# Padding every matmul of a fused attention and mixer kernel to the full TensorE array

## The chip, the cores and the metric

One core of a Trainium2 chip runs the program. The metric is the time of one execution on the device in microseconds (us). A TensorE matmul here is two instructions: a weight load of the stationary operand (`lhsT`; the profile's PEld, LDWEIGHTS) and a MATMUL that streams the moving operand (`rhs`) through the array. The profile writes the part of the array that an instruction uses as rows*columns: `128*64` is a stationary operand with 128 contraction rows and 64 columns.

## The reference

Batch 8, 8 heads, 576 positions, head size 64; then a mixer over positions of rank 32 and one over channels, 512 to 2048 to 512.

```python
cum  = np.cumsum(np.maximum(s, 0.0), axis=-1)
bias = -(cum[:, :, :, None] - cum[:, :, None, :])
scores = np.where(causal, -1e9, q @ k^T / sqrt(64) + np.minimum(bias, 0.0))
x = softmax(scores) @ v                       # heads side by side: (8, 576, 512)
u = x + (x.transpose(0, 2, 1) @ U @ V).transpose(0, 2, 1)   # U 576x32, V 32x576
out = u + np.maximum(u @ w_ch1, 0.0) @ w_ch2
```

## The kernel before

The 64 heads are worked in 32 pairs (four pairs a batch). The 576 positions make four key tiles of 128 and a tail tile of 64, which is where the part-filled arrays come from.

For pair n the program has these stages, each a generator that yields between pieces:

- `transposes(n+1)`: q and k (72 positions by 128 columns at a time) are transposed on TensorE (L159, stationary operand 72*128) into PSUM, and VectorE copies them into one of three `slot` tiles (L164). Four more rows of a slot, which carry the cumulative bias, come by DMA from `rows_hbm` (L151). A stationary operand of the scores has therefore 64 + 4 = 68 rows.
- `scores(n)`: for each of two heads nine matmuls (L180) make the score tiles transposed, keys on partitions: four diagonal blocks into `diag`, the tail block (keys and queries 512 to 575, stationary operand 68*64) into `tail`, and the blocks away from the diagonal into `far` and `mid`. ScalarE takes the exponential into `pT` (L191, L200, L204; L206 for both tails), VectorE masks the diagonal (L192, L212).
- `values(n-1)`: 15 matmuls a head (L235) multiply pT by v. v carries a 65th column of ones, so that the sums of the softmax come along. In the last row of blocks the one with j = 2 has a stationary operand of 128*64 and the one with j = 4 one of 64*64. VectorE divides (L244, L245) into `x_sb`.
- `seqmix(b)`, after each batch: U^T x in five matmuls (L259, stationary operand 128*32 four times, then 64*32), a copy to `ux` (L267), then x^T by multiplication with the identity (L272, 128*128) plus ux by V into the same PSUM tile (L280, 32*128), a copy to `uT` (L288); for the last 64 positions the same with 64*128 (L292) and 32*128 (L300) in turn, four of each, and L308.
- `chanmix(g)`, for 512 tokens: 64 matmuls 128x512 (L321), each four followed by a relu on ScalarE (L328), then 64 more (L334), the residual (L345), the copy out (L354) and the store. It is cut into pieces of four matmuls, 32 of them, and `step_fill` puts one piece behind each yield of the stages above: a pair gives 8 yields, `seqmix` 6 more a batch. Batch 0 has nothing to be filled with; the last two `chanmix` run alone at the end.

Loads of q, k, v and the weights (U_sb, V_sb, w1, w2) are DMAs issued by GpSimd in program order: q and k of batch 0, v of batch 0, all weights, then q, k and v of the next batches. At the very start GpSimd also fills constants (L68 to L100), and VectorE makes the bias rows out of s (L64 to L76), which go to HBM and back. PSUM tiles come from two pools of four, `pscore` and `pwork`. The order of each engine's instructions is fixed when the program is built.

Of the kernel before, what the change touches and what calls it, by code (L numbers as in the profile page):

```python
# [20 lines left out]
def kernel(  # L21
# [12 lines left out]
    nc = tc.nc  # L34
    B, H, S, D = q.shape
    assert (B, H, S, D) == (8, 8, 576, 64)
    DM = H * D
    FF = 4 * DM
    R = moe_U.shape[1]
    scale = 1.0 / (D ** 0.5)  # L40
    BH = B * H
# [4 lines left out]
    KA = D + 4  # L46
    NF = FF // 128

    consts = ctx.enter_context(tc.tile_pool(name="consts", bufs=1))
    loads = ctx.enter_context(tc.tile_pool(name="loads", bufs=2))  # L50
    work = ctx.enter_context(tc.tile_pool(name="work", bufs=2))
# [6 lines left out]
    def pwork():  # L58
        return ps_w.tile([128, 512], FP32, tag="w", name="pwork")


    s_sb = consts.tile([BH, S], FP32)
    nc.sync.dma_start(out=s_sb, in_=s.rearrange("b h s -> (b h) s"))
    nc.vector.tensor_scalar(s_sb, s_sb, 0.0, 1.0 / scale, op0=ALU.max, op1=ALU.mult)  # L64
    cum = consts.tile([BH, S], FP32)
    nc.vector.tensor_tensor_scan(cum, s_sb, s_sb, 0.0, op0=ALU.add, op1=ALU.max)
    rows = consts.tile([BH, 4, 2, S], BF16)
    nc.gpsimd.memset(rows[:, 0:3, 0, :], 1.0)  # L68
    nc.gpsimd.memset(rows[:, 3, 1, :], 1.0)
    rest = s_sb  # L70
# [6 lines left out]
    rows_hbm = nc.dram_tensor("rows_hbm", (4, BH, 2, S), BF16, kind="Internal").ap()  # L77
    nc.sync.dma_start(out=rows_hbm.rearrange("r n c s -> n r c s"), in_=rows)

    identity = consts.tile([128, 128], BF16)  # L80
    make_identity(nc, identity)

    keep = consts.tile([128, 4, 128], BF16)
    nc.gpsimd.memset(keep, 3.0e38)
    nc.gpsimd.affine_select(
        out=keep,
        in_=keep,
# [9 lines left out]
    v_slots = []  # L97
    for i in range(3):
        vt = consts.tile([128, 5, H, D + 1], BF16, name=f"v_slot{i}")
        nc.gpsimd.memset(vt[:, :, :, D : D + 1], 1.0)  # L100
        v_slots.append(vt)

    def load_qk(b, cuts):
# [22 lines left out]
    load_v(0)  # L126
    w1_sb = consts.tile([128, 4, FF], BF16)
    w2_sb = consts.tile([128, NF, DM], BF16)
    U_sb = consts.tile([128, 5, R], BF16)
    V_sb = consts.tile([R, S], BF16)  # L130

    def load_weights():
        nc.gpsimd.dma_start(
            out=U_sb[:, :4, :], in_=moe_U[:512].rearrange("(kt kp) r -> kp kt r", kp=128)
        )
        nc.gpsimd.dma_start(out=U_sb[:64, 4, :], in_=moe_U[512:576])
        nc.gpsimd.dma_start(out=V_sb, in_=moe_V)
        nc.gpsimd.dma_start(out=w1_sb, in_=moe_w_ch1.rearrange("(kt kp) n -> kp kt n", kp=128))
        nc.gpsimd.dma_start(out=w2_sb, in_=moe_w_ch2.rearrange("(kt kp) n -> kp kt n", kp=128))

    NSLOT = 3
    slots = [consts.tile([128, 2, 2, S], BF16, name=f"slot{i}") for i in range(NSLOT)]
    uT = consts.tile([128, 4, B * S], BF16)

    pT_of, x_of = {}, {}


    def transposes(n):
        b, hp = divmod(n, PB)
        slot = slots[n % NSLOT]  # L150
        nc.sync.dma_start(out=slot[D:KA], in_=rows_hbm[:, ds(2 * n, 2)])  # L151
        for hh in range(2):
            h = 2 * hp + hh
            tp = pwork().bitcast(BF16)[:, : 2 * 4 * TP].rearrange(
                "p (c t m) -> p c t m", c=2, t=4
            )
            for c, src in enumerate((q_t[b], k_t[b])):
                for t2 in range(4):
                    nc.tensor.transpose(  # L159
                        tp[:, c, t2, :], src[:, h, ds(t2 * 128, 128)], identity[:TP, :TP]  # L160
                    )
            dst = slot[0:D, hh].rearrange("p c (m t two) -> p c m t two", t=4, two=2)
            for par in range(2):
                nc.vector.tensor_copy(  # L164
                    dst[:, :, :, :, par],
                    tp[par * D : par * D + D].rearrange("p c t m -> p c m t"),
                )
            yield

    def scores(n):  # L170
        slot = slots[n % NSLOT]
        pT = work.tile([128, 2, 1600], BF16, tag="pT", name="pT")
        pT_of[n] = pT
        tail = pscore()
        for hh in range(2):
            qT = slot[0:KA, hh, 0, :]
            kT = slot[0:KA, hh, 1, :]

            def mm(dst, j, lo, hi):
                nc.tensor.matmul(  # L180
                    dst,
                    lhsT=kT[:, ds(j * 128, min(128, S - j * 128))],
                    rhs=qT[:, lo:hi],
                    start=True,
                    stop=True,
                )

            diag = pscore()
            for j in range(4):
                mm(diag[:, ds(j * 128, 128)], j, j * 128, j * 128 + 128)  # L190
            nc.scalar.activation(pT[:, hh, 0:512], diag, EXP, scale=scale)  # L191
            nc.vector.tensor_tensor(  # L192
                pT[:, hh, 0:512], pT[:, hh, 0:512], keep.rearrange("p a b -> p (a b)"), op=ALU.min
            )
            mm(tail[:64, ds(hh * 64, 64)], 4, 512, S)
            yield
            far = pscore()
            mm(far[:, 0:448], 0, 128, S)
            mm(far[:, 448:512], 3, 512, S)
            nc.scalar.activation(pT[:, hh, 512:1024], far, EXP, scale=scale)  # L200
            mid = pscore()
            mm(mid[:, 0:320], 1, 256, S)
            mm(mid[:, 320:512], 2, 384, S)
            nc.scalar.activation(pT[:, hh, 1024:1536], mid, EXP, scale=scale)  # L204
            if hh == 1:
                nc.scalar.activation(  # L206
                    pT[:64, :, 1536:1600],
                    tail[:64, 0:128].rearrange("p (a b) -> p a b", a=2),
                    EXP,
                    scale=scale,  # L210
                )
                nc.vector.tensor_tensor(  # L212
                    pT[:64, :, 1536:1600], pT[:64, :, 1536:1600], keep[:64, 0:2, 0:64], op=ALU.min
                )
            yield


    def place(j, i):
        if i == j:
            return 128 * j if j < 4 else 1536  # L220
        return {0: 512, 1: 1024, 2: 1344, 3: 960}[j] + 128 * (i - j - 1)

    def values(n):
        b, hp = divmod(n, PB)
        if hp == 0:
            x_of[b] = work.tile([128, 5, DM], BF16, tag="x_sb", name="x_sb")
        x_sb, pT, vt = x_of[b], pT_of.pop(n), v_slots[b % 3]
        for hh in range(2):
            h = 2 * hp + hh
            po = pwork()[:, : 5 * (D + 1)].rearrange("p (i d) -> p i d", i=5)  # L230
            for i in range(5):
                for j in range(i + 1):
                    kk = 64 if j == 4 else 128
                    mq = 64 if i == 4 and j in (2, 4) else 128
                    nc.tensor.matmul(  # L235
                        po[:mq, i, :],
                        lhsT=pT[:kk, hh, ds(place(j, i), mq)],
                        rhs=vt[:kk, j, h, :],
                        start=(j == 0),
                        stop=(j == i),  # L240
                        skip_group_check=True,
                    )
            rec = work.tile([128, 5, 1], FP32, tag="rec", name="rec", bufs=4)
            nc.vector.reciprocal(rec, po[:, :, D : D + 1])  # L244
            nc.vector.tensor_tensor(  # L245
                x_sb[:, :, ds(h * D, D)],
                po[:, :, 0:D],
                rec.to_broadcast([128, 5, D]),
                op=ALU.mult,
            )  # L250
            yield


    def seqmix(b):
        x_sb = x_of.pop(b)
        up = pwork()
        for t in range(5):
            kk = min(128, S - t * 128)
            nc.tensor.matmul(  # L259
                up[:R, :],  # L260
                lhsT=U_sb[:kk, t, :],
                rhs=x_sb[:kk, t, :],
                start=(t == 0),
                stop=(t == 4),
            )
        ux = work.tile([R, DM], BF16, tag="ux", name="ux")
        nc.vector.tensor_copy(ux, up[:R, :])  # L267
        yield
        for dt in range(4):
            ut = pwork()  # L270
            for t in range(4):
# [3 lines left out]
                    rhs=identity,  # L275
# [15 lines left out]
        for dt in range(4):  # L291
            nc.tensor.matmul(  # L292
                ut[:, ds(dt * 64, 64)],
                lhsT=x_sb[:64, 4, ds(dt * 128, 128)],
                rhs=identity[:64, :64],
                start=True,
                stop=False,
                skip_group_check=True,
            )
            nc.tensor.matmul(  # L300
                ut[:, ds(dt * 64, 64)],
                lhsT=ux[:, ds(dt * 128, 128)],
                rhs=V_sb[:, 512:S],
                start=False,
                stop=True,
                skip_group_check=True,
            )
# [116 lines left out]
```

## Time and profile before

| | |
|---|---|
| median of 3 runs | 488.96 us (487.77 to 490.62) |
| the profiled execution | 485.0 us, span 483.3 us |
| TensorE matmul busy | 452.3 us, 94% of the span, 3608 matmuls |
| VectorE busy | 232.1 us, 48% |
| ScalarE busy | 192.4 us, 40% |
| GpSimd busy | 58.9 us, 12% |
| mean granted TensorE clock | 0.982 of full speed |

Read it with care in one place: the end of a matmul is modelled and matmuls overlap, so the busy share of TensorE does not tell how much of the time data stream through the array. The distance from the start of one matmul to the start of the next tells more.

### The profile page before, as it was taken

To read this page: it belongs to the slowest core of one execution; us is meant where nothing else is said; L and a number is where in the kernel's file an instruction comes from. 1 tells how busy PE (TensorE), PEld (TensorE's weight loads), DVE (VectorE), ACT (ScalarE), POOL (GpSimd) and SP (SyncE) were. 2 spreads that over 40 slices of the span, in tenths; PEclk is the share of its full clock that TensorE was granted. 3 is DMA by queue.
4 is the path that set the end of the run, shared out by engine and by line. 5 is a ranking of instruction groups with operands and counts; after the bars stand their busy time and mean duration, and the time that the engine had idled before them with its cause. 6 is when DMAs were issued, how large, how long until landed. Compare 5 with 4: busy or idle time off the path is not lost.

```text
span 483.3 us, 8414 instructions
## 1 busy us (share of the span) xinstructions
PE 452.3 (94%) x3608; PEld 255.9 (53%) x3608; DVE 232.1 (48%) x444; ACT 192.4 (40%) x369; POOL 58.9 (12%) x80
## 2 busy tenths in 40 slices
PE   1195999999999999999999999999999999999996
PEld 1073645555555555555556555555555555444443
DVE  6363755555455544556455644555555543401101
ACT  1064236532562266324742165326632662061430
POOL 9720341003000301021100310000000000000000
PEclk9999999999999989998999799999999999999999
DMA  5999996518071536127431806110011000101101
GB/s 83 189 210 191 111 127 31 83 55 87 3 101 46 72 25 88 37 54 64 60 67 46 72 4 99 46 46 2 3 47 46 1 0 24 45 22 45 43 23 65
DMA packets 59221, 29.74 MB, mean 62 GB/s; under 512 B 42320, under 2 KB 53616, under 8 KB 59184
## 3 DMA queue, kind: packets, MB, share of 16 engines
q0 software_dynamic: 53392, 18.44, 45.3%
q1 hardware_dynamic: 5792, 10.77, 6.4%
q8 instruction: 28, 0.46, 0.4%
q14 instruction: 9, 0.07, 0.1%
HBM read 37.58 MB, written 10.03 MB: 99 GB/s over the span
## 4 chain that ended last, share of the span: by engine, by line
PE 89%; DMA 7%; POOL 2%; DVE 1%; issue 0%; POOLq 0%
PE pwork L321 28%; PE pwork L334 27%; PE pscore L180 11%; PE pwork L235 10%; DMA q_sd<-in_q_dram 6%; PE pwork L159 3%; PE pwork L259 2%; PE pwork L272 2%; PE pwork L280 2%; PE pwork L345 2%; DMA v_slot_93<-in_v_dram 2%; PE pwork L292 1%; PE pwork L300 1%; POOL k_sd L109 1%; POOL q_sd L109 1%
## 5 line engine op out<-in xcount | busy, mean ns | idle before, releaser
L321 PE MATMUL pwork<-uT,w_sb 128*128 128x512 bf16 x576 | 146.7, 391 | 0.0
L334 PE MATMUL pwork<-w_sb,hT 128*128 128x512 bf16 x576 | 144.4, 380 | 0.0
L328 ACT ACTIVATE hT<-pwork 128x512 bf16<-128x512 f32 x144 | 86.4, 600 | 106.1 <-PE pwork L321 105.5
L191 ACT ACTIVATE pT<-pscore 128x512 bf16<-128x512 f32 x64 | 38.4, 600 | 145.8 <-issue 89.5
L321 PEld LDWEIGHTS <-w_sb 128*128 128x128 bf16 x576 | 52.1, 100 | 51.2 <-issue 5.0
L334 PEld LDWEIGHTS <-hT 128*128 128x128 bf16 x576 | 49.2, 98 | 45.2 <-issue 1.1
L235 PEld LDWEIGHTS <-pT 128*128 128x128 bf16 (+2 forms) x960 | 54.3, 102 | 24.0 <-issue 0.4
L354 DVE COPY o_sb<-pwork 128x512 f32<-128x512 f32 x36 | 24.9, 692 | 75.7 <-PE pwork L345 75.7
L244 DVE RECIPROCAL rec<-pwork 128x5 f32<-128x5 f32 x64 | 12.3, 195 | 87.5 <-PE pwork L235 87.3
L192 DVE TENSOR_TENSOR pT<-pT,keep 128x512 bf16<-128x512 bf16 x64 | 26.3, 414 | 47.5 <-ACT pT L191 47.5
L200 ACT ACTIVATE pT<-pscore 128x512 bf16<-128x512 f32 x64 | 38.1, 595 | 20.0 <-PE pscore L180 19.0
L180 PE MATMUL pscore<-slot_118 68*128 68x128 bf16 (+5 forms) x198 | 28.5, 266 | 10.7 <-DMA slot_118<-rows_hbm 10.7
L204 ACT ACTIVATE pT<-pscore 128x512 bf16<-128x512 f32 x64 | 38.2, 597 | 0.3 <-PE pscore L180 0.2
L164 DVE COPY slot_119<-pwork 64x576 bf16<-64x576 bf16 x44 | 35.1, 799 | 6.2 <-PE pwork L159 4.6
L164 DVE COPY slot_118<-pwork 64x576 bf16<-64x576 bf16 x44 | 35.2, 799 | 4.5 <-PE pwork L159 3.1
L159 PE MATMUL pwork<-identity,q_sd 72*128 72x72 bf16 x256 | 20.9, 213 | 15.4 <-DMA q_sd<-in_q_dram 15.4
L164 DVE COPY slot_120<-pwork 64x576 bf16<-64x576 bf16 x40 | 32.0, 801 | 4.4 <-PE pwork L159 3.1
L159 PEld LDWEIGHTS <-q_sd 72*128 72x128 bf16 x256 | 17.4, 108 | 27.8 <-DMA q_sd<-in_q_dram 16.1
L245 DVE TENSOR_TENSOR x_sb<-pwork,rec 128x320 bf16<-128x320 f32 x64 | 31.1, 490 | 2.0
L180 PE MATMUL pscore<-slot_119 68*128 68x128 bf16 (+5 forms) x198 | 28.6, 263 | 0.8 <-DVE slot_119 L164 0.8
L180 PEld LDWEIGHTS <-slot_118 68*128 68x128 bf16 (+1 forms) x198 | 16.5, 105 | 23.0 <-issue 12.4
L235 PE MATMUL pwork<-v_slot_93,pT 128*128 128x65 bf16 (+1 forms) x360 | 27.2, 214 | 0.0
(59 smaller groups left out, 333.9 us busy)
## 6 DMA issues: line engine op xcount, KB each, us to landing
out_dram<-o_sb SPq DMA_DIRECT2D x36, 256.0 KB
w_sb<-in_moe_w_ch_dram POOLq DMA_DIRECT2D x2, 2048.0 KB, 19.6
q_sd<-in_q_dram POOLq DMA_DIRECT2D x7, 576.0 KB, 7.9
k_sd<-in_k_dram POOLq DMA_DIRECT2D x7, 576.0 KB, 11.0
v_slot_93<-in_v_dram POOLq DMA_DIRECT2D x12, 128.0 KB, 7.8
v_slot_95<-in_v_dram POOLq DMA_DIRECT2D x12, 128.0 KB, 6.1
v_slot_97<-in_v_dram POOLq DMA_DIRECT2D x8, 128.0 KB, 9.1
q_sd<-in_q_dram POOLq DMA_DIRECT2D x4, 144.0 KB, 5.0
```

The costliest lines, as they stand in the source:

```text
L159: nc.tensor.transpose(tp[:, c, t2, :], src[:, h, ds(t2 * 128, 128)], identity[:TP, :TP])
L164: nc.vector.tensor_copy(dst[:, :, :, :, par], tp[par * D : par * D + D].rearrange("p c t m -> p c m t"),)
L180: nc.tensor.matmul(dst, lhsT=kT[:, ds(j * 128, min(128, S - j * 128))], rhs=qT[:, lo:hi], start=True, stop=True,)
L191: nc.scalar.activation(pT[:, hh, 0:512], diag, EXP, scale=scale)
L192: nc.vector.tensor_tensor(pT[:, hh, 0:512], pT[:, hh, 0:512], keep.rearrange("p a b -> p (a b)"), op=ALU.min)
L200: nc.scalar.activation(pT[:, hh, 512:1024], far, EXP, scale=scale)
L204: nc.scalar.activation(pT[:, hh, 1024:1536], mid, EXP, scale=scale)
L235: nc.tensor.matmul(po[:mq, i, :], lhsT=pT[:kk, hh, ds(place(j, i), mq)], rhs=vt[:kk, j, h, :], start=(j == 0), stop=(j == i), skip_group_c ...
L245: nc.vector.tensor_tensor(x_sb[:, :, ds(h * D, D)], po[:, :, 0:D], rec.to_broadcast([128, 5, D]), op=ALU.mult,)
L321: nc.tensor.matmul(f1, lhsT=w1_sb[:, kt, ds(nf * 128, 128)], rhs=uT[:, kt, ds(g * 512, 512)], start=(kt == 0), stop=(kt == 3),)
L328: nc.scalar.activation(hT[:, nf, :], f1, RELU)
L334: nc.tensor.matmul(f2, lhsT=hT[:, nf, ds(i * 128, 128)], rhs=w2_sb[:, nf, :], start=(nf == 0), stop=False, skip_group_check=True,)
```

## The change

Every stationary operand becomes one of more than 64 rows and 128 columns; the missing part is padded.

- Scores: the k half of a slot grows from 576 to 640 columns (`SK`), the last 64 zeroed once. The tail matmul takes 128 key columns, fills 128 partitions of `tail`, and the exponential and the mask of the tail work on 128 partitions instead of 64. The rows 64 to 127 are masked to zero.
- AV: `pT` becomes two fixed tiles with 64 more columns (`PW`), set once; every stationary operand is 128 columns wide, and v has its missing 64 rows zeroed once (on GpSimd), so that j = 4 contracts over 128 rows. What lands in the partitions 64 to 127 of the last block row is not used.
- `seqmix`: U is padded with zeros to 128 columns and 640 rows, V to 128 rows; `ux` has 128 rows.
- Space: `s_sb`, `cum` and `rows` move into a buffer of the `hT` pool (`early`).

The number of matmuls and the moving sizes (65, 64, 512 columns) stay.

```diff
-    s_sb = consts.tile([BH, S], FP32)
+    early = work.tile([128, NF, 512], BF16, tag="hT", name="hT").rearrange("p a b -> p (a b)")
+    s_sb = early[:BH, 8 * S : 10 * S].bitcast(FP32)
...
+        nc.gpsimd.memset(vt[64:, 4, :, :], 0.0)
...
-    U_sb = consts.tile([128, 5, R], BF16)
-    V_sb = consts.tile([R, S], BF16)
+    U_sb = consts.tile([128, 5, 128], BF16)
+    nc.vector.memset(U_sb, 0.0)
+    V_sb = consts.tile([128, S], BF16)
+    nc.vector.memset(V_sb, 0.0)
...
-    slots = [consts.tile([128, 2, 2, S], BF16, name=f"slot{i}") for i in range(NSLOT)]
+    SK = 5 * 128
+    slots = [consts.tile([128, 2, S + SK], BF16, name=f"slot{i}") for i in range(NSLOT)]
+    for slot in slots:
+        nc.vector.memset(slot[:KA, :, 2 * S :], 0.0)
+    PW = 1664
+    pTs = [consts.tile([128, 2, PW], BF16, name=f"pT{i}") for i in range(2)]
+    for pT in pTs:
+        nc.vector.memset(pT[:, :, 1600:], 1.0)
...
-                    lhsT=kT[:, ds(j * 128, min(128, S - j * 128))],
+                    lhsT=kT[:, ds(j * 128, 128)],
...
-            mm(tail[:64, ds(hh * 64, 64)], 4, 512, S)
+            mm(tail[:, ds(hh * 64, 64)], 4, 512, S)
...
-                    kk = 64 if j == 4 else 128
-                    mq = 64 if i == 4 and j in (2, 4) else 128
-                        po[:mq, i, :],
-                        lhsT=pT[:kk, hh, ds(place(j, i), mq)],
-                        rhs=vt[:kk, j, h, :],
+                        po[:, i, :],
+                        lhsT=pT[:, hh, ds(place(j, i), 128)],
+                        rhs=vt[:, j, h, :],
...
-                up[:R, :],
-                lhsT=U_sb[:kk, t, :],
-                rhs=x_sb[:kk, t, :],
+                up,
+                lhsT=U_sb[:, t, :],
+                rhs=x_sb[:, t, :],
...
-        ux = work.tile([R, DM], BF16, tag="ux", name="ux")
-        nc.vector.tensor_copy(ux, up[:R, :])
+        ux = work.tile([128, DM], BF16, tag="ux", name="ux")
+        nc.vector.tensor_copy(ux, up)
...
-                lhsT=x_sb[:64, 4, ds(dt * 128, 128)],
-                rhs=identity[:64, :64],
+                lhsT=x_sb[:, 4, ds(dt * 128, 128)],
+                rhs=identity[:, :64],
```

After the first two pairs TensorE has its instructions in the same order as before; only sizes differ. This is TensorE at the end of one head's AV in batch 1, before the change. Each row ends with the size that the matmul writes, partitions by columns.

```order
L235 MATMUL pwork<-v_slot_95,pT 128x65
L235 LDWEIGHTS pT
L235 MATMUL pwork<-v_slot_95,pT 64x65
L235 LDWEIGHTS pT
L235 MATMUL pwork<-v_slot_95,pT 128x65
L235 LDWEIGHTS pT
L235 MATMUL pwork<-v_slot_95,pT 64x65
L334 LDWEIGHTS hT
```

And the same place after it (L246 is the former L235, L344 the former L334):

```order
L246 MATMUL pwork<-v_slot_94,pT_128 128x65
L246 LDWEIGHTS pT_128
L246 MATMUL pwork<-v_slot_94,pT_128 128x65
L246 LDWEIGHTS pT_128
L246 MATMUL pwork<-v_slot_94,pT_128 128x65
L246 LDWEIGHTS pT_128
L246 MATMUL pwork<-v_slot_94,pT_128 128x65
L344 LDWEIGHTS hT
```

Nothing moved; the second and the fourth matmul write all 128 partitions now.

GpSimd at the start, before: after the columns of ones come the loads of batch 0.

```order
L100 MEMSET v_slot_93 128x40
L100 MEMSET v_slot_95 128x40
L100 MEMSET v_slot_97 128x40
L109 DMA q_sd<-in_q_dram 72x2x512
L109 DMA k_sd<-in_k_dram 72x2x512
```

And after:

```order
L102 MEMSET v_slot_91 128x40
L102 MEMSET v_slot_94 128x40
L102 MEMSET v_slot_97 128x40
L112 DMA q_sd<-in_q_dram 72x2x512
L103 MEMSET v_slot_91 64x520
L103 MEMSET v_slot_94 64x520
L103 MEMSET v_slot_97 64x520
L112 DMA k_sd<-in_k_dram 72x2x512
```

Three fills stand between the first load of q and all later DMAs of GpSimd's queue. VectorE likewise gets seven fills (U_sb, V_sb, three slots, two pT) ahead of its first instruction on s.

More of the change, by code (lines that the diff above doesn't have):

```diff
@@ L59, in pwork @@
         return ps_w.tile([128, 512], FP32, tag="w", name="pwork")
-    s_sb = consts.tile([BH, S], FP32)
+    early = work.tile([128, NF, 512], BF16, tag="hT", name="hT").rearrange("p a b -> p (a b)")
+    s_sb = early[:BH, 8 * S : 10 * S].bitcast(FP32)
     nc.sync.dma_start(out=s_sb, in_=s.rearrange("b h s -> (b h) s"))
     nc.vector.tensor_scalar(s_sb, s_sb, 0.0, 1.0 / scale, op0=ALU.max, op1=ALU.mult)
-    cum = consts.tile([BH, S], FP32)
+    cum = early[:BH, 10 * S : 12 * S].bitcast(FP32)
     nc.vector.tensor_tensor_scan(cum, s_sb, s_sb, 0.0, op0=ALU.add, op1=ALU.max)
-    rows = consts.tile([BH, 4, 2, S], BF16)
+    rows = early[:BH, : 8 * S].rearrange("p (r c s) -> p r c s", r=4, c=2)
     nc.gpsimd.memset(rows[:, 0:3, 0, :], 1.0)
@@ L128 @@
     w2_sb = consts.tile([128, NF, DM], BF16)
-    U_sb = consts.tile([128, 5, R], BF16)
-    V_sb = consts.tile([R, S], BF16)
+    U_sb = consts.tile([128, 5, 128], BF16)
+    nc.vector.memset(U_sb, 0.0)
+    V_sb = consts.tile([128, S], BF16)
+    nc.vector.memset(V_sb, 0.0)
     def load_weights():
         nc.gpsimd.dma_start(
-            out=U_sb[:, :4, :], in_=moe_U[:512].rearrange("(kt kp) r -> kp kt r", kp=128)
+            out=U_sb[:, :4, :R], in_=moe_U[:512].rearrange("(kt kp) r -> kp kt r", kp=128)
         )
-        nc.gpsimd.dma_start(out=U_sb[:64, 4, :], in_=moe_U[512:576])
-        nc.gpsimd.dma_start(out=V_sb, in_=moe_V)
+        nc.gpsimd.dma_start(out=U_sb[:64, 4, :R], in_=moe_U[512:576])
+        nc.gpsimd.dma_start(out=V_sb[:R], in_=moe_V)
         nc.gpsimd.dma_start(out=w1_sb, in_=moe_w_ch1.rearrange("(kt kp) n -> kp kt n", kp=128))
@@ L141 @@
     NSLOT = 3
-    slots = [consts.tile([128, 2, 2, S], BF16, name=f"slot{i}") for i in range(NSLOT)]
+    SK = 5 * 128
[6 more added lines that the diff above has]
+        nc.vector.memset(pT[:, :, 1600:], 1.0)
     uT = consts.tile([128, 4, B * S], BF16)
-    pT_of, x_of = {}, {}
+    x_of = {}
     def transposes(n):
@@ L150, in transposes @@
         slot = slots[n % NSLOT]
-        nc.sync.dma_start(out=slot[D:KA], in_=rows_hbm[:, ds(2 * n, 2)])
+        nc.sync.dma_start(out=slot[D:KA, :, 0 : 2 * S], in_=rows_hbm[:, ds(2 * n, 2)].rearrange("r n c s -> r n (c s)"))
         for hh in range(2):
@@ L161, in transposes @@
                     )
-            dst = slot[0:D, hh].rearrange("p c (m t two) -> p c m t two", t=4, two=2)
+            dst = slot[0:D, hh, 0 : 2 * S].rearrange("p (c m t two) -> p c m t two", c=2, t=4, two=2)
             for par in range(2):
@@ L171, in scores @@
         slot = slots[n % NSLOT]
-        pT = work.tile([128, 2, 1600], BF16, tag="pT", name="pT")
-        pT_of[n] = pT
+        pT = pTs[n % 2]
         tail = pscore()
         for hh in range(2):
-            qT = slot[0:KA, hh, 0, :]
-            kT = slot[0:KA, hh, 1, :]
+            qT = slot[0:KA, hh, 0:S]
+            kT = slot[0:KA, hh, S:]
             def mm(dst, j, lo, hi):
@@ L206, in scores @@
                 nc.scalar.activation(
-                    pT[:64, :, 1536:1600],
-                    tail[:64, 0:128].rearrange("p (a b) -> p a b", a=2),
+                    pT[:, :, 1536:1600],
+                    tail[:, 0:128].rearrange("p (a b) -> p a b", a=2),
                     EXP,
@@ L212, in scores @@
                 nc.vector.tensor_tensor(
-                    pT[:64, :, 1536:1600], pT[:64, :, 1536:1600], keep[:64, 0:2, 0:64], op=ALU.min
+                    pT[:, :, 1536:1600], pT[:, :, 1536:1600], keep[:, 0:2, 0:64], op=ALU.min
                 )
@@ L226, in values @@
             x_of[b] = work.tile([128, 5, DM], BF16, tag="x_sb", name="x_sb")
-        x_sb, pT, vt = x_of[b], pT_of.pop(n), v_slots[b % 3]
+        x_sb, pT, vt = x_of[b], pTs[n % 2], v_slots[b % 3]
         for hh in range(2):
@@ L257, in seqmix @@
         for t in range(5):
-            kk = min(128, S - t * 128)
             nc.tensor.matmul(
-                up[:R, :],
-                lhsT=U_sb[:kk, t, :],
-                rhs=x_sb[:kk, t, :],
+                up,
+                lhsT=U_sb[:, t, :],
+                rhs=x_sb[:, t, :],
                 start=(t == 0),
```

## Prediction

> **What bounds the kernel now.** I read the page first (busy time, slices, the chain that ended last), then the waits, then the timeline around places where the array's shape changes.
>
> ```profile
> PE 452.3 (94%) x3608; PEld 255.9 (53%) x3608; DVE 232.1 (48%) x444; ACT 192.4 (40%) x369; POOL 58.9 (12%) x80
> PE   1195999999999999999999999999999999999996
> PE 89%; DMA 7%; POOL 2%; DVE 1%; issue 0%; POOLq 0%
> PE pwork L159 <- DMA q_sd<-in_q_dram: 15.4, 3, 8.3
> PE pscore L180 <- DMA slot_118<-rows_hbm: 10.7, 1, 10.7
> PE pscore L180 <- DVE slot_119 L164: 0.8, 1, 0.8
> ```
>
> TensorE has work in every slice from the fifth on, the chain runs through it for 89%, and its waits are for first loads: 15.4 us for q and 10.7 us for bias rows. Behind 48.7 us the only wait left is one of 0.8 us. So what shortens the distance between two matmul starts shortens the kernel. Two pieces of the timeline show what that distance is, first for one head's AV (L235), 15 matmuls of 65 columns:
>
> ```profile
> 109.35 0.53 PE L235 MATMUL pwork<-v_slot_95,pT 128*128 128x65 bf16 x12
> 109.80 0.50 PE L235 MATMUL pwork<-v_slot_95,pT 128*64 128x65 bf16 x3
> 110.23 0.39 PE L334 MATMUL pwork<-w_sb,hT 128*128 128x512 bf16 x1
> ```
>
> A single small matmul is shown 0.20 us long, so the first twelve start (0.53 - 0.20) / 11 = 0.03 us apart. The last of them starts at 109.35 + 0.33 = 109.68; the next start, 128*64, is at 109.80, and from there three steps (to 128*128, to 64*64, to the next 128*128) take 0.43 us. Four steps with a change of array shape take 0.55 us where four without take 0.12: **0.43 us a head, about 0.11 us a change of shape**. Nothing is waited for there. The scores of one head next:
>
> ```profile
> 103.83 0.54 PE L180 MATMUL pscore<-slot_120 68*128 68x128 bf16 x5
> 104.30 0.39 PE L334 MATMUL pwork<-w_sb,hT 128*128 128x512 bf16 x1
> 108.04 0.60 PE L180 MATMUL pscore<-slot_120 68*128 68x448 bf16 x4
> 108.48 0.38 PE L334 MATMUL pwork<-w_sb,hT 128*128 128x512 bf16 x1
> 101.71 0.29 PE L159 MATMUL pwork<-identity,k_sd 72*128 72x72 bf16 x4
> 101.84 0.38 PE L334 MATMUL pwork<-w_sb,hT 128*128 128x512 bf16 x1
> ```
>
> The lower pairs are the control. Four matmuls of 68*128 with 448 + 64 + 320 + 192 = 1024 columns take 0.44 us, 0.43 ns a column, and are followed by 128*128 with no charge; nor do 72 rows cost any (four in 0.13 us). So 68 or 72 rows count as full. The upper pair, four diagonal blocks and the tail of 68*64, has 576 columns, 0.25 us by that rate, and takes 0.47: **0.22 us for each tail**.
>
> The Trainium skill, "TensorEngine Tiling (Array Packing)", section "Key Properties", says that switching the tiling mode drains TensorE, without a duration; the trace agrees, with 0.11 us. Its section "The Solution" speaks against padding: operands of up to 64 rows or columns could run side by side, up to twice as fast. No row here shows two small tiles side by side (L292 and L300 below, 64 and 32 rows, start 0.13 us apart), so that use is not lost; were it had, those eight would take some 0.11 us in place of 0.22, and the sum would be better by the old layout by 0.1 us a batch.
>
> **The change, part by part.** One `seqmix` (batch 1):
>
> ```profile
> 112.93 0.33 PE L345 MATMUL pwork<-identity,uT 128*128 128x128 bf16 x3
> 113.19 1.35 PE L259 MATMUL pwork<-x_sb,U_sb 128*32 128x512 bf16 x5
> 114.48 0.29 PE L272 MATMUL pwork<-identity,x_sb 128*128 128x128 bf16 x2
> ...
> 116.12 0.40 PE L272 MATMUL pwork<-identity,x_sb 128*128 128x128 bf16 x4
> 116.45 0.38 PE L280 MATMUL pwork<-V_sb,ux 32*128 32x512 bf16 x1
> 116.76 0.20 PE L292 MATMUL pwork<-identity,x_sb 64*128 64x64 bf16 x1
> 116.89 0.20 PE L300 MATMUL pwork<-V_sb,ux 32*128 32x64 bf16 x1
> ```
>
> By the column rate 512 columns are 0.22 us, 128 are 0.055, 64 are 0.028. Into L259: about 0.15 us from the last L345 start for a 0.055 step, 0.09 over. L259: 1.29 us for 1.08, 0.21 over. L272 to L280 0.33 for 0.22 and L280 to L292 0.31 for 0.22: 0.20 a round, two rounds a batch (12 + 3 and 4 + 1 matmuls), 0.40. The eight L292 and L300 in turn, 0.13 us a step: 1.04 for 0.22, 0.82. Sum 1.52 us a `seqmix`.
>
> *From the first `seqmix` (63.3 us) to the end*, where no wait hides anything: pairs 0 to 3 have had their AV and pairs 0 to 5 their scores by then, which leaves 56 heads of AV x 0.43 = 24.1 us, 52 tails x 0.22 = 11.4 us, 8 `seqmix` x 1.52 = 12.2 us. Together **-47.7 us**.
>
> *Before 63.3 us* the padding gains little:
>
> ```profile
> 20.44 28.22 DMA q_sd<-in_q_dram
> 48.70 0.66 PE L159 MATMUL pwork<-identity,q_sd 72*128 72x72 bf16 x8 [5.63 <-DMA q_sd<-in_q_dram]
> 52.57 3.23 DVE L164 COPY slot_119<-pwork 64x576 bf16<-64x576 bf16 x4
> 55.84 3.27 DVE L164 COPY slot_120<-pwork 64x576 bf16<-64x576 bf16 x4
> 63.34 2.43 PE L259 MATMUL pwork<-x_sb,U_sb 128*32 128x512 bf16 x5
> 2.28 0.57 POOL L69 MEMSET rows<- 64x576 bf16 x1
> 3.53 1.74 DVE L64 TENSOR_SCALAR s_sb<-s_sb 64x576 f32<-64x576 f32 x1 [3.53 <-DMA s_sb<-in_s_dram]
> ```
>
> At 48.7 us TensorE waits for q of batch 1, behind all weights: a shorter stretch before it only lengthens that wait. From 48.7 to 63.3 there are four heads of AV and four to six tails, 4 x 0.43 + 5 x 0.22 = 2.8 us of changes, but VectorE copies without a break from 52.6 to 59.1, so I take 1.8 (0.5 to 2.8). Against it stand GpSimd's three fills of 64x520, put ahead of nearly all its DMAs: by the row of 64x576 (0.57 us) 0.5 each, 1.5 us at most, 0 if the DMA engines have a queue of their own to work off; I take 1.2, nearest the row, since the chain to 48.7 us starts with GpSimd. Net **-0.6 us** (+1 to -2.8). VectorE's seven fills have its idle first 3.5 us, in which it waits for s; were they longer than that, the 5.6 us wait at 48.7 would cover it.
>
> Nothing else has a price: exponential, mask and `ux` copy work on more partitions with the same free size, the DMAs carry the same bytes, and the fixed `pT` tiles alternate as the pool's two buffers did.
>
> **The clock.**
>
> ```profile
> 115.30:118.70 3.40, 3.40 (x33) 1.90 (x31) 2.82 (x5) 0.51 (x1) 0.85 (x2) 1.00 1.87 181
> 118.70:122.20 3.50, 3.50 (x22) 1.74 (x19) 2.34 (x3) 1.77 (x4) 0.00 (x0) 0.51 0.39 23
> 119.03 1.91 PE L321 MATMUL pwork<-uT,w_sb 128*128 128x512 bf16 x4
> 100.48 1.04 PE L334 MATMUL pwork<-w_sb,hT 128*128 128x512 bf16 x4
> core 0: 483.3 us, clock 0.982
> ```
>
> Right behind the `seqmix` whose small matmuls stand 0.13 us apart, the granted clock is half for one stretch of 3.4 us (the 0.51 near the second row's end), and four matmuls take 1.91 us in place of 1.04. A mean of 0.982 means 2 x 0.018 x 483.3 = 17.4 us at half clock, 8.7 us lost. With the changes of shape gone, the stretch ahead, now 3.4 us, holds denser work, and I expect four of five such dips to go: **-7 us** (0 to -8.7).
>
> **New waits.** The stretch that was TensorE's alone gets tighter:
>
> ```profile
> 67.50:412.00 344.50, 344.50 (x2915) 196.73 (x2914) 185.79 (x362) 151.31 (x294) 27.39 (x33) 0.98 0.37 48
> 115.79 2.49 DVE L288 CAST uT<-pwork 128x512 bf16<-128x512 f32 x4 [0.53 <-PE pwork L280]
> L328 ACT ACTIVATE hT<-pwork 128x512 bf16<-128x512 f32 x144 | 86.4, 600 | 106.1 <-PE pwork L321 105.5
> L200 ACT ACTIVATE pT<-pscore 128x512 bf16<-128x512 f32 x64 | 38.1, 595 | 20.0 <-PE pscore L180 19.0
> L206 ACT ACTIVATE pT<-pscore 64x128 bf16<-64x128 f32 x32 | 8.5, 267 | 0.0
> ```
>
> VectorE has 186 and ScalarE 151 of 344.5 us; in some 295 us they are at 63% and 51%. In `seqmix` the four L288 copies (2.49 us) free the `pwork` tiles that the next transposes need; TensorE arrives there 1.0 us sooner than before and would wait some 0.35 us for each of 7: **+2.5 us** (0 to +8).
>
> **Sum.** 485.0 - 47.7 - 0.6 - 7 + 2.5 = 432.2 us against the profiled execution, which ran 4.0 us below the median of 488.96. Its difference to the timed runs may be two or three more dips of the clock (1.7 us each), which would go too, or a constant; I add 1 us and predict **433 us**, itself from 424 to 439.
>
> **Rivals.**
> - *The clock goes on dipping.* The Trainium skill, "TensorE: Matmul & The Clock Gate", Part 1, gives half rate only after a whole idle window of some 3.4 us. By that rule the dips would not hang on small gaps and would stay; the trace has dips with no such idle stretch, which speaks against it. As a mechanism of this kernel: the copies of L288 hold TensorE back in `seqmix` as long as the changes of shape did, so the stretch stays as thin. Then 7 us come back: 440 us. 14%.
> - *ScalarE takes over where the relu runs.* A pair there has eight L328 of 0.6 us, six exponentials of 0.6 and one of 0.27, 8.7 us. TensorE's pair is eight fills of 0.88 and, a head, 1600 columns of scores (0.69), 15 AV (0.45) and eight transposes (0.26): 8 x 0.88 + 2 x 1.40 = 9.8 us without changes of shape, 11.1 with them. At 89% an in-order engine can hold up `pscore`; 0.8 us in each of 16 such pairs gives 13 us: 446 us. Against it: ScalarE is under 60% over a batch and `pwork` has four tiles. 10%.
> - *The gap is not of the shape* but of small operands as such, or of what the tail matmuls wait for; then nothing changes: 488 us. The control rows (64 columns after 448 without charge) speak against it. 4%.
> - *Slower:* the fuller array makes the clock dip all through. Each dip of 3.4 us costs 1.7; 28 of them, 96 us of the span at half clock, eat the whole gain, and half the span would give some 530 us. The full-array stretch at the end shows none. 2%.
>
> **How the numbers follow.** Forecast 68%, rivals 14, 10, 4 and 2; 2% for under 424. About 0.5% is what a measurement of this kernel can tell from no change. Faster are all but the last two rivals: 0.95; same 0.03; slower 0.02. A range of 423 to 448 us holds the forecast and the first two rivals and leaves out the rest with the tails of the forecast.
>
> **What the profile after would show.** Every stationary operand of L193, L246, L269, L290, L302 and L310 as 68*128 or 128*128; 15 AV matmuls to the next stage in about 0.45 us in place of 0.88; four diagonal blocks and tail in 0.25; L302 and L310 0.03 us apart; about 43 us from one batch's L269 to the next; a clock near 0.995. The forecast is wrong if the step of 0.11 us shows up between equal shapes, or if TensorE's waits for L298, L338 or the exponentials sum to more than 10 us.

## The result

| | before | after |
|---|---|---|
| median | 489.79 us (487.77 to 491.22, 4 runs) | 431.37 us (430.94 to 432.27, 4 runs) |
| span of the profiled execution | 483.3 us | 429.4 us |
| ratio | | 0.8812, 95% interval 0.8774 to 0.885 |

The forecast was 433 us, in a range of 423 to 448. The lines of the page of the changed kernel that answer to those of before: busy time, slices of TensorE, granted clock, the chain that ended last.

```profile
PE 390.8 (91%) x3608; PEld 229.5 (53%) x3608; DVE 232.9 (54%) x451; ACT 191.4 (45%) x369; POOL 60.4 (14%) x83
PE   0168289999999999999999999999999999999996
PEclk9999558999999999999999999999999999999999
PE 85%; DMA 9%; POOL 3%; DVE 1%; issue 1%; POOLq 0%
```

There are the same 3608 matmuls, and TensorE still works without a break from the seventh slice on. Where the time went shows in the timeline, at the places that the prediction read (start, duration, engine, line, tiles, shape, count; dots stand for rows left out): one head's AV, one head's diagonal blocks and tail, the end of a mixer.

```profile
106.50 0.63 PE L246 MATMUL pwork<-v_slot_94,pT_128 128*128 128x65 bf16 x15
106.96 1.03 PE L344 MATMUL pwork<-w_sb,hT 128*128 128x512 bf16 x4
...
100.11 0.42 PE L193 MATMUL pscore<-slot_123 68*128 68x128 bf16 x5
100.36 0.81 PE L344 MATMUL pwork<-w_sb,hT 128*128 128x512 bf16 x3
...
110.96 0.38 PE L290 MATMUL pwork<-V_sb,ux 128*128 128x512 bf16 x1
111.25 0.19 PE L302 MATMUL pwork<-identity,x_sb 128*128 128x64 bf16 x1
111.28 0.19 PE L310 MATMUL pwork<-V_sb,ux 128*128 128x64 bf16 x1
```

The 15 AV matmuls take 0.46 us in place of 0.88, blocks and tail 0.25 in place of 0.47, and L302 and L310 follow at 0.03 us in place of 0.13. From L290 to L302 there are 0.29 us where 512 columns need 0.22: a short wait that is new.

The whole is best read from the distance between two batches, the start of L259 (L269 after) in the chain. First come two starts before, with no drop of the clock between them, then two after:

```profile
320.63 1.28 PE pwork L259 x5
370.43 1.28 PE pwork L259 x5
```

```profile
151.49 1.08 PE pwork L269 x5
194.77 1.08 PE pwork L269 x5
```

49.80 us became 43.28, so 6.52 us a batch. The first mixer (L259, after L269) starts at 63.34 us before and at 64.16 after: nothing was won ahead of it. From there to the end it is 420.0 us before and 365.2 after.

### The profile page after: what moved, and what is told of

It reads as the page before. It is cut to its first block, busy times and chain, and to the rows that moved or that the text cites. A ratio compares the mean times of both kernels' runs of the same rounds, so it can differ in the third digit from the quotient of the medians.

```text
span 429.4 us, 8600 instructions
## 1 busy us (share of the span) xinstructions
PE 390.8 (91%) x3608; PEld 229.5 (53%) x3608; DVE 232.9 (54%) x451; ACT 191.4 (45%) x369; POOL 60.4 (14%) x83
## 4 chain that ended last, share of the span: by engine, by line
PE 85%; DMA 9%; POOL 3%; DVE 1%; issue 1%; POOLq 0%
PE pwork L331 29%; PE pwork L344 29%; PE pscore L193 10%; DMA k_sd<-in_k_dram 7%; PE pwork L246 6%; PE pwork L173 3%; PE pwork L269 2%; DMA v_slot_91<-in_v_dram 2%; PE pwork L355 2%; PE pwork L282 2%; PE pwork L290 2%; POOL k_sd L112 1%; POOL v_slot_91 L120 1%; POOL q_sd L112 1%; DVE uT L298 0%
## 5 line engine op out<-in xcount | busy, mean ns | idle before, releaser
L344 PE MATMUL pwork<-w_sb,hT 128*128 128x512 bf16 x576 | 143.8, 379 | 0.0
L331 PE MATMUL pwork<-uT,w_sb 128*128 128x512 bf16 x576 | 140.5, 379 | 0.2 <-DVE uT L298 0.2
L338 ACT ACTIVATE hT<-pwork 128x512 bf16<-128x512 f32 x144 | 87.6, 608 | 77.8 <-PE pwork L331 77.3
L331 PEld LDWEIGHTS <-w_sb 128*128 128x128 bf16 x576 | 51.1, 98 | 46.9 <-issue 0.3
L344 PEld LDWEIGHTS <-hT 128*128 128x128 bf16 x576 | 50.2, 98 | 42.6
L204 ACT ACTIVATE pT_127<-pscore 128x512 bf16<-128x512 f32 x32 | 19.3, 602 | 74.9 <-PE pscore L193 74.9
L204 ACT ACTIVATE pT_128<-pscore 128x512 bf16<-128x512 f32 x32 | 19.1, 597 | 53.1 <-PE pscore L193 53.0
L173 PE MATMUL pwork<-identity,q_sd 72*128 72x72 bf16 x256 | 19.9, 206 | 18.6 <-DMA q_sd<-in_q_dram 18.4
L193 PE MATMUL pscore<-slot_121 68*128 68x128 bf16 (+4 forms) x198 | 24.5, 255 | 9.9 <-DMA slot_121<-rows_hbm 9.8
L173 PEld LDWEIGHTS <-q_sd 72*128 72x128 bf16 x256 | 16.8, 104 | 29.5 <-DMA q_sd<-in_q_dram 18.8
L205 DVE TENSOR_TENSOR pT_127<-pT_127,keep 128x512 bf16<-128x512 bf16 x32 | 13.1, 413 | 25.9 <-ACT pT_127 L204 25.9
L193 PE MATMUL pscore<-slot_122 68*128 68x128 bf16 (+4 forms) x198 | 25.3, 259 | 0.9 <-DVE slot_122 L178 0.7
L193 PEld LDWEIGHTS <-slot_121 68*128 68x128 bf16 x198 | 15.4, 104 | 19.3 <-issue 10.8
L173 PE MATMUL pwork<-identity,k_sd 72*128 72x72 bf16 x256 | 19.6, 208 | 5.2 <-DMA k_sd<-in_k_dram 5.2
L246 PEld LDWEIGHTS <-pT_127 128*128 128x128 bf16 x480 | 20.5, 102 | 6.9 <-issue 0.2
L246 PEld LDWEIGHTS <-pT_128 128*128 128x128 bf16 x480 | 20.4, 102 | 7.0
```

What stands on the lines that cost most here:

```text
L173: nc.tensor.transpose(tp[:, c, t2, :], src[:, h, ds(t2 * 128, 128)], identity[:TP, :TP])
L193: nc.tensor.matmul(dst, lhsT=kT[:, ds(j * 128, 128)], rhs=qT[:, lo:hi], start=True, stop=True,)
L205: nc.vector.tensor_tensor(pT[:, hh, 0:512], pT[:, hh, 0:512], keep.rearrange("p a b -> p (a b)"), op=ALU.min)
L246: nc.tensor.matmul(po[:, i, :], lhsT=pT[:, hh, ds(place(j, i), 128)], rhs=vt[:, j, h, :], start=(j == 0), stop=(j == i), skip_group_check= ...
L331: nc.tensor.matmul(f1, lhsT=w1_sb[:, kt, ds(nf * 128, 128)], rhs=uT[:, kt, ds(g * 512, 512)], start=(kt == 0), stop=(kt == 3),)
L338: nc.scalar.activation(hT[:, nf, :], f1, RELU)
```

## The experiments

Each was timed against the kernel before on the same chip; medians of the kernel before were 489.6 us (first four), 487.3 (next four) and 487.8 (last two). The changed kernel's 431.37 us come from another round, in which the kernel before took 489.79, so a distance from it is uncertain by some 2 us; where it matters, the distance of the ratios is given too. A *dip* is a stretch at half the granted clock. Edits are shown in part, dots for lines left out.

**e1: the mixer alone.** Of the change only U, V, `ux` and the last 64 positions are padded. Against the changed kernel, tails and AV are undone:

```diff
-            mm(tail[:, ds(hh * 64, 64)], 4, 512, S)
+            mm(tail[:64, ds(hh * 64, 64)], 4, 512, S)
...
-                        po[:, i, :],
-                        lhsT=pT[:, hh, ds(place(j, i), 128)],
-                        rhs=vt[:, j, h, :],
+                        po[:mq, i, :],
+                        lhsT=pT[:kk, hh, ds(place(j, i), mq)],
+                        rhs=vt[:kk, j, h, :],
```

> Only the operands of the position mixer (U, V, ux, the last 64 positions) are padded; AV and the score tails stay part-filled. Theory (each change of array shape costs about 0.11 us, and the clock dips because the mixer's small matmuls make its stretch thin): 8 x 1.5 us = 12 us from the steps and most of the 8.7 us of the dips, so 489.8 - 12 - 8 = 470 us, with no stretch of half clock after the first 68 us. Rival (the dips come and go with the phase of the batch period against a window of 3.4 us, not with the mixer's density): 12 us less only, 478 us, dips in some batches still. Rival (the step is a price of small operands, not of a change): 490 us.

Measured: 469.0 us, ratio 0.9569 (0.9511 to 0.9626). Cores view, and two batches of the chain:

```profile
core 0: 466.9 us, clock 1.000
```

```profile
163.35 1.08 PE pwork L270 x5
211.84 1.08 PE pwork L270 x5
```

That is 20.6 us less. A batch without a dip is 49.80 - 48.49 = 1.31 us shorter, 10.5 us over eight, and in all four runs no granted clock below full is on record. From the first mixer (65.59 us here) to the end it takes 401.3 us in place of 420.0: the 18.7 us are the 10.5 of the steps and 8.2 more, about what 17 us at half clock had cost before. That a price hangs on the part-filled operands is settled, but not whether on each of them or on the change between them, since padding removes both; e4 separates the two.

**e2: AV alone.** Tails and mixer are as before. Against the changed kernel:

```diff
-    U_sb = consts.tile([128, 5, 128], BF16)
-    nc.vector.memset(U_sb, 0.0)
-    V_sb = consts.tile([128, S], BF16)
-    nc.vector.memset(V_sb, 0.0)
+    U_sb = consts.tile([128, 5, R], BF16)
+    V_sb = consts.tile([R, S], BF16)
...
-            mm(tail[:, ds(hh * 64, 64)], 4, 512, S)
+            mm(tail[:64, ds(hh * 64, 64)], 4, 512, S)
...
-                lhsT=x_sb[:, 4, ds(dt * 128, 128)],
-                rhs=identity[:, :64],
+                lhsT=x_sb[:64, 4, ds(dt * 128, 128)],
+                rhs=identity[:64, :64],
```

> Only the AV operands are padded (fixed pT tiles, zeroed v rows); score tails and mixer stay part-filled. Theory: 56 heads x 0.43 us = 24 us less, 1 us back for the three fills on GpSimd: 467 us. The mixer's rest stage stays at 0.13 us a matmul. If the dips hang on the thin mixer they stay, in those batches whose mixer fills a whole window of 3.4 us; if they were luck of the period they may go or grow, 459 to 470 us. Rival (the price is of small operands): 490 us.

Measured: 465.2 us, ratio 0.9501 (0.945 to 0.9552). A batch without a dip takes 46.25 us here, 3.55 less, 0.44 a head (expected 0.43). The mixer is as thin as before, and the clock drops behind it, but not each time. Stretches of the trace, with busy time of the five engines and then the granted clock, DMA share and GB/s; L268 starts at 254.3 us in one batch and at 303.7 in the next:

```profile
254.30:258.90 4.60, 4.60 (x36) 2.41 (x35) 3.39 (x6) 0.00 (x0) 3.38 (x5) 1.00 1.31 129
258.90:265.70 6.80, 6.80 (x35) 3.36 (x35) 4.29 (x7) 2.88 (x5) 0.00 (x0) 0.50 0.70 40
303.70:308.30 4.60, 4.60 (x37) 2.43 (x35) 3.36 (x6) 0.00 (x0) 0.00 (x0) 1.00 0.15 57
308.30:311.70 3.40, 3.40 (x34) 2.02 (x34) 3.11 (x5) 2.31 (x5) 0.00 (x0) 1.00 0.02 5
```

TensorE has the same work in both, once with 6.8 us at half clock behind it and once without. So a thin mixer alone doesn't make a dip. Nor do the loads, which run in the upper pair (GpSimd busy, DMA 1.31) and not in the lower: the mixer at 350.0 us has none (DMA 0.16) and a dip of 6.8 us behind it, the one at 112.3 us has them (1.27) and no dip.

**e3: the score tails alone.** Against the kernel before:

```diff
-                    lhsT=kT[:, ds(j * 128, min(128, S - j * 128))],
+                    lhsT=kT[:, ds(j * 128, 128)],
...
-            mm(tail[:64, ds(hh * 64, 64)], 4, 512, S)
+            mm(tail[:, ds(hh * 64, 64)], 4, 512, S)
```

> Only the score tails are padded to 128 key columns; AV and mixer stay. Theory: 52 tails x 0.22 us = 11 us less: 478 us, and diagonal blocks plus tail in 0.25 us instead of 0.47. Rival (price of small operands, or the 128-row exponential costs more): 490 us or above.

Measured: 470.5 us, ratio 0.9588 (0.9512 to 0.9663), more than the 11 us expected.

```profile
100.80 0.42 PE L190 MATMUL pscore<-slot 68*128 68x128 bf16 x5
101.05 1.03 PE L344 MATMUL pwork<-w_sb,hT 128*128 128x512 bf16 x4
```

The step is as expected, 0.25 us for blocks and tail. Batches without a dip are 48.02 us apart, 1.78 less, 14 us over eight batches if all had a tail left to win, 11 for the 52 tails counted. The trace has only two dips behind the first mixer (3.4 us each) where that of before had 17 us at half clock, which is worth some 5 us. With the 11 for the tails that leaves about 3 of the 19 us won, inside the 7 us over which these runs spread.

**e4: no padding, fewer changes of shape.** In the kernel before the last stage of the mixer is written as four L292, then four L300. The instructions are the same in number and size; in this order the last 64 positions do not come out as the reference's, so this is a probe and not a version to use. Against the kernel before:

```diff
                 skip_group_check=True,
             )
+        for dt in range(4):
             nc.tensor.matmul(
                 ut[:, ds(dt * 64, 64)],
```

> The kernel before, nothing padded; in the mixer's last stage the four 64*128 matmuls come first and then the four 32*128, instead of in turn. The same instructions, but three changes of array shape in place of nine. Theory (price per change): 6 x 0.105 x 8 = 5 us less, 485 us, with L292 and then L300 0.03 us apart inside each four. Rival (price per part-filled operand): no difference, 490 us, 0.13 us a step still. A denser stretch may also take some of the dips away, up to 8 us more.

Measured: 475.5 us, ratio 0.9698 (0.964 to 0.9756).

```profile
168.90 0.29 PE L292 MATMUL pwork<-identity,x_sb 64*128 64x64 bf16 x4
169.12 0.29 PE L301 MATMUL pwork<-V_sb,ux 32*128 32x64 bf16 x4
169.34 0.73 PE L180 MATMUL pscore<-slot 68*128 68x128 bf16 x4
```

Four matmuls of one part-filled shape and the change to the next take 0.22 us; before, four such steps took 0.52. Part-filled operands run at 0.03 us inside a group. **The price is paid for the change of shape, not for the small operand.** Nor is it paid for two matmuls in a row into the same PSUM columns, which grouping also takes away: in the changed kernel L302 and L310 keep taking turns and stand 0.03 us apart. For operands with few columns the kernel before has the control itself: its four L259 of 128\*32 start 0.22 us apart, as 512 columns do behind a full operand. Batches of e4 follow each other at 49.18 us, 0.62 less than 49.80: six changes of 0.103. That is 5 us over eight; the granted clock is 0.999 to 1.000 in the four runs, and the other 9 us again are about what dips cost before.

**e5: the mixer undone.** The changed kernel with the mixer's operands part-filled again (U_sb, V_sb, `ux` and x_sb as in e2).

> The changed kernel with the mixer alone put back to part-filled operands (AV and score tails stay padded). Theory: 8 x 1.5 us of changes of shape come back and with them the thin stretch in which the clock can dip: 431.4 + 12 = 443.5 us with no dip, up to 452 with a dip of 3.4 to 6.8 us at half clock in every batch. If the dips need a thin mixer and the right phase of the free-running window, their number differs from the kernel before (batches now follow each other at 44.8 us in place of 51.4). Rival (padding the mixer's small part is worth nothing once the rest is padded): 431 us.

Measured: 444.7 us, ratio 0.9093 (0.9026 to 0.916), runs from 441.0 to 448.9: 13 us above the changed kernel. A batch takes 44.47 us without a dip, 1.19 more. The trace has three dips of 3.4 us, 5 us in all; a run of 442.0 us has a granted clock of 1.000 on record. By the batch the mixer's padding is worth nearly what it was worth alone (1.19 and 1.31 us); in the whole less, 13 us against 20.6, in part since fewer dips came back than had gone.

**e6: the fills on VectorE.** Against the changed kernel:

```diff
-        nc.gpsimd.memset(vt[64:, 4, :, :], 0.0)
+        nc.vector.memset(vt[64:, 4, :, :], 0.0)
```

> The changed kernel with the three fills of v rows done by VectorE at its idle start in place of GpSimd between its first DMAs. Theory (these fills push GpSimd's queue, and with it the landing of q and k of batch 1, back by 1.4 us): the loads of batch 1 land 1.5 to 3 us earlier, 431.4 - 1.5 = 430 us, at best 428.5. Rival (the DMA engines are the limit there, so that the queue's delay is worth nothing): 431.4 us.

Measured: 429.7 us, ratio 0.8799 (0.8761 to 0.8836), 1.65 us less than the changed kernel's median (0.6 by the ratios), within overlapping intervals. Its trace does not bear out the theory: the start of the work on batch 1's q moved, that on its k hardly. After, then e6:

```profile
50.38 0.66 PE L173 MATMUL pwork<-identity,q_sd 72*128 72x72 bf16 x8 [9.13 <-DMA q_sd<-in_q_dram]
55.01 0.90 PE L173 MATMUL pwork<-identity,k_sd 72*128 72x72 bf16 x12 [1.91 <-DMA k_sd<-in_k_dram]
```

```profile
49.46 0.66 PE L173 MATMUL pwork<-identity,q_sd 72*128 72x72 bf16 x8 [10.09 <-DMA q_sd<-in_q_dram]
54.80 0.90 PE L173 MATMUL pwork<-identity,k_sd 72*128 72x72 bf16 x12 [2.61 <-DMA k_sd<-in_k_dram]
```

Work on k starts 0.2 us earlier, not 1.5 to 3. The run does not decide between theory and rival.

**e7: loads of batch 1 first.** Against the changed kernel:

```diff
         nc.gpsimd.dma_start(out=w1_sb, in_=moe_w_ch1.rearrange("(kt kp) n -> kp kt n", kp=128))
+        load_v(1)
         nc.gpsimd.dma_start(out=w2_sb, in_=moe_w_ch2.rearrange("(kt kp) n -> kp kt n", kp=128))
...
     drain(transposes(0))
+    load_qk(1, 1)
     load_weights()
...
-        if hp == 0 and b + 1 < B:
+        if hp == 0 and 0 < b < B - 1:
```

> The changed kernel with q and k of batch 1 loaded ahead of the weights, and v of batch 1 between the two large weights. Theory (up to the first mixer the kernel waits for those loads, so the padding gains nothing there): the waits of 9.1 and 1.9 us at 41 to 55 us go, the first mixer starts some 10 us earlier, and the weights still land before they are needed: 421 us (419 to 424). Rival (the first large weight becomes the wait in their place): 427 to 432 us.

Measured: 418.7 us, ratio 0.8583 (0.8544 to 0.8623), 12.7 less than the changed kernel (11.2 by the ratios). Waits of TensorE (in total, times, longest), after and e7, and then the first mixer of e7 in its timeline:

```profile
PE pwork L173 <- DMA q_sd<-in_q_dram: 18.4, 3, 9.1
```

```profile
PE pwork L174 <- DMA q_sd<-in_q_dram: 8.7, 2, 8.3
```

```profile
50.97 2.29 PE L270 MATMUL pwork<-x_sb,U_sb 128*128 128x512 bf16 x5 [0.40 <-DVE x_sb L257]
```

The wait of 9.1 us for batch 1 is gone; what is left is for batch 0. The first mixer starts at 50.97 us in place of 64.16, 13.2 earlier, and waits for VectorE alone, and the weights are no new wait; the time is even a little below the expected stretch. The stretch ahead of the first mixer was bound by these loads, as the prediction had it.

**e8: both,** the edits of e6 and e7.

> Both of the last two edits. Theory: the wait for batch 1 is gone by the order of the loads, so the fills only shift the start of the first loads: 0.5 to 1.5 us on top, 420 us (418 to 423). If the fills had counted only through the wait for batch 1, the same as with the order of loads alone.

Measured: 416.6 us, ratio 0.8534 (0.8487 to 0.8581): the fastest version, 14.8 us below the changed kernel and 15% below the kernel before. It lies below the expected stretch; the step from e7 is 2.1 us, with overlapping intervals, so that what the fills alone are worth stays open.

**e9: the kernel before again**, for a second trace.

> The kernel before once more, for a second trace. Theory (a dip comes when a window of 3.41 us begins 1 to 2.6 us behind the start of a batch's L259 and so holds the thin part of the mixer; a batch with a dip takes 51.4 us, almost 15 windows of 3.413, so that the next batch meets the window at nearly the same place and dips come in runs): every dip begins 4.5 to 6.2 us behind an L259 start, in 3 to 6 batches, mostly in a row; batches without a dip follow each other at 49.8 us, those with one at 51.4. Rival (a dip in every thin mixer, or at other places): dips in all eight, or away from the mixer.

Measured: 486.8 us. Stretches from the start of the mixers at 217.9 and 320.7 us on:

```profile
217.90:222.60 4.70, 4.70 (x39) 2.51 (x37) 3.48 (x6) 0.00 (x0) 2.94 (x4) 1.00 1.53 142
222.60:229.40 6.80, 6.80 (x34) 3.25 (x35) 4.19 (x7) 2.88 (x5) 0.00 (x0) 0.50 0.47 31
320.70:325.40 4.70, 4.70 (x39) 2.51 (x37) 3.47 (x6) 0.00 (x0) 0.00 (x0) 1.00 0.15 56
325.40:329.00 3.60, 3.60 (x34) 2.06 (x35) 3.30 (x6) 2.68 (x5) 0.00 (x0) 1.00 0.02 5
```

Dips stand 5.0, 4.8 and 5.7 us behind three L259 starts (and one 7.1 behind the first, in the stage that starts at half clock); four of the other mixers, as thin, have none. The expected distance of 4.5 to 6.2 us held for three of the four dips, the expected row of neighbours for two. In the first trace the second to fifth mixers dipped, here the first, third, fourth and seventh: the same program dips in different batches from run to run, at about the same distance from the mixer.

**e10: shifted phase.** Four more dense matmuls in each `chanmix`. Against the kernel before:

```diff
-            for kt in range(4):
+            for kt in [0, 1, 2, 3] * (2 if nf == 8 else 1):
```

> The kernel before with four more dense matmuls in each chanmix (one group of L321 done twice), far from the mixer: 0.86 us more work in each of nine. Batches then follow each other at 50.7 us without a dip (14.8 windows) and 52.3 with one (15.3), so a dip throws the next mixer out of phase. Theory: dips in 1 to 3 of the mixers, never in two consecutive batches, each 4.5 to 6.2 us behind an L259 start; 7.7 us more work less 1 to 3 dips of 1.7: 492 to 496 us. Rival (dips hang on the thin mixer alone): as many dips as before, in a row, and 7.7 us more, 497 us.

Measured: 498.8 us (491.3 to 500.3), ratio 1.0131 (1.002 to 1.0243).

```profile
175.30:182.10 6.80, 6.80 (x34) 3.26 (x35) 4.19 (x7) 2.88 (x5) 0.00 (x0) 0.50 0.62 38
229.90:233.30 3.40, 3.40 (x23) 1.74 (x20) 2.09 (x3) 1.85 (x4) 0.00 (x0) 0.51 0.36 22
282.30:285.70 3.40, 3.40 (x29) 1.77 (x26) 3.21 (x5) 2.51 (x6) 0.00 (x0) 1.00 0.42 24
```

L259 starts at 170.6, 224.5 and 276.8 us. The place was right (4.7 and 5.4 us behind, and in all five dips of this trace 4.7 to 5.9), the count wrong: five mixers dipped, not one to three, and consecutive ones. In this execution a dip does not throw the next mixer out of phase. The times do not decide: the median is nearer the rival's 497 us, but runs go down to 491.3, and the interval of the ratio runs from 1 to 12 us more.

## Why the prediction was right

*The bound* was right: TensorE's starts set the time from the first mixer on, and each part of the padding shortened a batch by nearly its own price.

*The price of a change of shape* was right to a few per cent. Behind the first mixer 47.7 us were forecast, 6.72 a batch by its terms. Measured batch distances give 3.55 for AV, 1.78 for tails and 1.31 for the mixer, 6.64 together, and 6.52 with all three. e4 shows the cause, which the prediction had only from control rows: the same small matmuls, grouped, lose the price. For AV and tails only padding was run; that their price too is one of the change rests on its equal size of 0.11 us. The rival "not of the shape" is out.

*New waits* were put at 0.35 us a mixer, for `pwork` tiles that the copies of L298 free. The size was right, the place only in part. In the mixer at 108.05 us four steps take longer than their columns: L193 to L290 by 0.17 us, L290 to L302 by 0.07, L193 to L173 by 0.04 and L193 to L331 by 0.09, together 0.37, and the next five mixers repeat them.

```profile
109.33 0.69 DVE L277 CAST ux<-pwork 128x512 bf16<-128x512 f32 x1 [0.39 <-PE pwork L269]
110.08 0.82 PE L290 MATMUL pwork<-V_sb,ux 128*128 128x512 bf16 x3
110.50 2.48 DVE L298 CAST uT<-pwork 128x512 bf16<-128x512 f32 x4 [0.48 <-PE pwork L290]
```

The last three of these starts come 0.05 us behind the end of a copy of L298, as forecast. The first comes 0.06 us behind the end of L277, the copy to `ux` that L290 reads, and this wait the sum had put at nothing. That the total still came out is luck. The waits also account for the mixer's smaller yield: e1 has only the first two, and 1.52 - 0.24 = 1.28 us is near its 1.31; with all four 1.15 would be left, near the 1.19 of e5. Behind the first mixer TensorE has no wait for ScalarE on record: its rival is out.

*The clock*: four of five dips were to go, -7 us. All went, 17.1 us at half clock and thus 8.5 us. Two stretches of the changed kernel, the clock in the third number from the end:

```profile
62.70:67.40 4.70, 4.70 (x27) 2.94 (x26) 2.86 (x9) 2.67 (x6) 1.57 (x2) 0.50 2.55 129
67.40:360.00 292.60, 292.20 (x2922) 172.27 (x2920) 185.53 (x362) 150.84 (x294) 28.49 (x34) 1.00 0.45 58
```

The mean of 0.972 after, below the 0.982 of before, comes from the stage ahead of 67.4 us alone, which ran at half clock before too, with the record not yet begun; the forecast of a mean near 0.995 overlooked that. As to the reason, the prediction's was half the story. Dips need the thin mixer: none begins behind a mixer in the traces with a denser one (after, e1, e6 to e8, and e4, whose mixer is 0.62 us shorter). They need something more (e2 and e9: as thin, and often none). That this is a window which falls on the thin part is argued from the lengths and places of the dips and not shown. Rival one, that they would stay, is out. The Trainium skill, "TensorE: Matmul & The Clock Gate", Part 1, "What's actually happening", has a free-running window of 3413 ns; the lengths of 3.4 and 6.8 us agree. The table in that section of the Trainium skill lists half rate after an idle window (that it comes only then is the prediction's word); these dips do not agree, since TensorE shows no wait ahead of them. Counted from the rise at 67.4 us in steps of 3.413, a window would end 4.8 us behind the mixer at 151.3, the place where dips came, and there is none, which suggests that the phase no longer matters with a dense mixer.

*Ahead of the first mixer* the forecast was -0.6 us; the traces gave +0.8. What failed here is the reading of single landings as fixed. e9, the kernel before, has its first mixer at 65.37 us where the first trace had 63.34, since k of batch 1 landed 2 us later. Against that spread neither the padding's gain nor the price of GpSimd's fills (taken as 1.2 us) is told apart, and e6 does not settle it. Right was that nothing would be won there; e7 shows what it hangs on.

*The step from the profiled execution to the median* (+1 us) was a guess. The profiled execution of before stood 4.8 us below the median of four runs, the one of after 0.3 below its own: in the traces before spreads by dips and first loads, the padded kernels only by the first stage. The sum of 432.2 us against 431.06 in the profiled execution is 1.1 off, with errors that partly cancel (-1.5 on the clock, +1.4 ahead of the mixer, the rest on the steps), so its closeness is in part luck. Of the chances, all but the last two rivals add up to 0.94 and not 0.95.

## What to carry to other kernels

In a stream of matmuls that binds, look for neighbours whose stationary operands fill different parts of the array, and take the distance from start to start, not the busy share: here 500 such changes of some 0.11 us hid in a TensorE that looked 94% busy. Pad the odd ones to the common shape, or where that can't be and the accumulation allows it, group them (e4). Look apart at what lies ahead of the first dense stretch, where padding won nothing and the order of the first loads won 11 to 13 us.

## What the runs showed of the hardware

- A change between 128-row, 64-row and 32-row or between 128-, 64- and 32-column operands cost 0.09 to 0.12 us each on top of the columns streamed; 68 and 72 rows counted as full.
- A full weight load and a matmul of 65 columns together came every 0.03 us, the step of the grouped operands with 64 and 32 rows in e4 (64 columns): the fuller load cost nothing.
- The granted clock went to half for 3.4 or 6.8 us while TensorE had no idle gap on record, 4.5 to 6 us behind the start of a thin mixer (6 to 7 behind the first one), in some executions and batches and not in others. What exactly is counted in a window stays open.
- The clock column reads 1.00 where its record has not begun: five L259 took 2.43 us at 63.3 us of before under a 1.00.
